# Dilated sliding-window attention and a two-layer MLP: the last four plain output tiles join the groups of seven products, three loads change their queue, and the order is made anew

## The chip, the core and the metric

The kernel runs on one core of a Trainium2 chip. Five engines work side by side and meet at semaphores: TensorE (PE in the profile, its weight loads PEld), VectorE (DVE), ScalarE (ACT), GpSimd (POOL) and SyncE (SP), which here only issues transfers. PE multiplies out of SBUF into eight PSUM banks; DVE and ACT read PSUM, POOL does not. Transfers between HBM and SBUF are carried by 16 DMA engines and are issued by SP or ACT. The metric is the device time of one launch in microseconds.

## The reference

Two stages, with float32 inputs and output. Stage one is attention over 8 batches, 8 heads, 576 tokens and 64 dimensions. Heads 0 to 3 see a window of the last 32 tokens; heads 4 to 7 see every fourth token of the last 128.

```python
scores = scale * q @ k.T                     # per batch and head, 576 x 576
mask_plain = (rel >= 0) & (rel < 32)
mask_dil = (rel >= 0) & (rel < 128) & (rel % 4 == 0)
attn = softmax(where(mask, scores, -1e9)) @ v
```

Stage two takes the 8 x 576 = 4608 tokens with 8 x 64 = 512 features each: `h = x @ w_in` (512 x 2048), `g = max(0.01 h, h)`, `out = g @ w_out` (2048 x 512).

## The kernel before

All operands are cast to fp16 on the chip. The tokens of two batches (1152) are cut into three chunks of 384, so there are 12 chunks, and each chunk has three output tiles of 128 tokens: 36 tiles.

**Attention.** The heads of a batch are handled in pairs, called `vi` 0 to 3; 2 and 3 are the dilated ones and go first (`VISITS`). For batches 0 and 1, q and k are loaded into `stg`, cast into `nat` (L501 on ACT, L502 on DVE or POOL), transposed on PE (L740) and copied into `slots` (L513, L514). v is loaded into `vst` and cast into `slots`. A `unit` (two per pair) multiplies scores (L896, the mask as a bias by L892), takes the exponential on ACT (L904), sums on PE (L921), multiplies with v (L915), takes 1/sum on ACT as a logarithm and an exponential (L940, L942) and normalises on DVE into `xt` (L953). Each unit takes two PSUM banks. The last 64 tokens of a batch go through a buffer `rest` of their own (transposes at L788, `rest_unit`).

**First layer.** `up` (L1054) and `up_pair` (L1088) multiply `w_in` with `xt`, and ACT writes the leaky ReLU into `gt` (L1070). Chunk 0 goes block by block: the products of one head pair can run as soon as that pair's rows of `w_in` and of `xt` are there. Chunk 1 is half batch 0 (first 192 tokens) and half batch 1. The last three chunks (9 to 11) use seven products for eight (`ups7`, L1188).

**Second layer.** It has two forms. `down` makes a plain tile: 16 matmuls of 512 columns (L1268) in four parts, each part waiting only for its four rows of `w_out`; DVE copies the result out (L1276). `group` makes four tiles by Strassen's scheme in Winograd's form: seven products of two halves, each eight matmuls of 256 columns (L1358), with eight sums of activations on DVE (L1344), copies out of PSUM on ACT or DVE (L1387, L1389) and additions on DVE (L1395). It needs four sums of weight blocks (`weight_sums`, L1298), made once when all of `w_out` has been cast; the third overwrites a block of `w_out` in place. The sums of activations use `rest` and `pair1` as buffers; `half_free[0]` makes the first group wait until the transposes of batch 0's and 1's rests have read `rest`:

```python
half_free[0] = raw[0, "rest"][1] + raw[1, "rest"][1]
part_free[0] = part_free[1] = rings["STG"][-1]
```

`PLAIN` says how many tiles are plain before the groups begin: 4, so that there are four plain tiles and eight groups.

**What sets the order.** The kernel first collects all work as tasks with their dependencies and modelled durations (`_Plan`). A forward pass places them on engines and queues by priority; a backward pass from the end gives each its latest start as its new priority; this is repeated `PASSES` times. Then a table `NUDGE` shifts the priorities of single tasks (by task number), and a table `HAND` pins single tasks to an engine. The instructions are written out in the order that results, and each engine runs its own in order. `LATE`, `FAST` and the like are terms of the modelled arrival of transfers; `WHEN` holds first guesses for the times of the batches.

The opening is written out by hand in `FIRST`, a list of steps: `q01` loads q and k of batch 0's head group 1 (heads 4 to 7), `v01` its v, `r0` the rests, `w0` to `w15` the sixteen 512 KB blocks of weights (0 to 7 are `w_in`, 8 to 15 are `w_out`), `c` a mask table. The priority of such a load is the place of its step in the list, shifted by `NUDGE`. Nearly all loads are issued by SP (L486); ACT issues k of `q01` and the identity (`con`). The casts of a weight block go to POOL or DVE, or to ACT as well for the blocks listed in `HELPED`, which is empty. Where PE has nothing to do before its first MLP product, the program fills the planned gap with products of zeros (`warm`, L1472 and L1589).

Of the kernel before, what the change touches and what calls it, by code (L numbers as in the profile page):

```python
# [15 lines left out]
ROOM, LATE, LANDS, SERVE, FSERVE = 256, 1.06, 0.6, 1.1, 1.04  # L16
SOON = 0
FAST = 0.21
WHEN = (3.92, 2.82, 39.64, 80.18, 115.4, 117.81, 161.72, 152.03)
PASSES = 8  # L20
SEVEN = (9, 10, 11)
SECOND = 'st01t'
# [3 lines left out]
HELPED = ()  # L26
TURNS, SCORES, SUMS_, VALUES, UPS, DOWNS = 0, 0, 0, 0, 0, 0
STRETCH = 1.0
FIRST = ('r0 q01 q00 v01 v00 w0 w1 w2 w3 w4 w5 w6 q11 w7 w8 q10 w9 w10 v11 w11 w12 w13 w14 v10 '
         'w15 r1 c')  # L30
NUDGE = {
# [334 lines left out]
def kernel(  # L366
# [14 lines left out]
    B, H, S, D = q.shape  # L381
# [45 lines left out]
    VH = 1152  # L427
# [190 lines left out]
    def load_v(b, g, prio, queue="SP"):  # L618
        base = (b * H + 4 * g) * HS
        vn, v_old = ring("VST", NVS, v_users := [])  # L620
        vs, v_old = vst[vn], v_old + t_blank[vn]
# [26 lines left out]
    w_in_t, w_out_t = {}, {}  # L648
# [1003 lines left out]
```

## Time and profile before

| | us |
|---|---|
| median of 3 runs | 294.82 (294.46 to 295.19) |
| profiled execution, its own time | 296.16 |
| its span | 294.4 |
| PE busy | 284.7 (97%) |
| DVE busy | 225.3 (77%) |
| ACT busy | 218.5 (74%) |
| POOL busy | 124.2 (42%) |

The span runs from the first to the last instruction, so the profiled execution has 1.8 us around it. PE's busy time includes the products of zeros at the start. Rows of a timeline read: start, duration, engine, line of the kernel, operation, what it writes and reads, how many were merged; in brackets the idle time of the engine just before, and what ended it. A row of a stage reads: length, then busy time and count of instructions for each engine, the granted clock of PE as a share, the mean busy share of the 16 DMA engines (a little above 1 when packets overlap), and GB/s.

### The profile page before, as it was taken

How to read it: one execution, taken by the hardware profiler on the slowest of the kernel's cores; microseconds unless marked ns; L12 is line 12 of the kernel's file. 1: busy time of each engine (PE TensorE's matmuls, PEld its weight loads, DVE VectorE, ACT ScalarE, POOL GpSimd, SP SyncE). 2: the span in 40 equal slices, each digit the busy share in tenths (PEclk: the TensorE clock that was granted, in tenths of full speed). 3: DMA queues.
4: the chain of work that ended last, by engine and by line, in shares of the span. 5: the costliest groups of instructions: out<-in, count | busy, mean ns of one | idle time of the engine just before them, and what ended most of it. 6: DMA issues, size and time to landing. Idle time of an engine off the chain costs nothing.

```text
span 294.4 us, 7619 instructions
## 1 busy us (share of the span) xinstructions
PE 284.7 (97%) x2920; PEld 226.3 (77%) x2920; DVE 225.3 (77%) x437; ACT 218.5 (74%) x482; POOL 124.2 (42%) x174
## 2 busy tenths in 40 slices
PE   6879999999999999999999999999999999999995
PEld 2557776686687789677777787887688999999984
DVE  7858397864799879867839879897878889678672
ACT  4967898489859985888978887988767965755521
POOL 4540452656537747874873683653424000000000
PEclk9979999999999999999999999999999999999999
DMA  7999999799788969999798898852001210121133
GB/s 240 275 403 401 394 366 203 156 175 208 128 169 185 170 150 186 199 157 199 198 178 142 195 182 153 197 134 75 31 7 36 75 38 0 38 73 36 38 108 109
DMA packets 156068, 47.15 MB, mean 160 GB/s; under 512 B 136832, under 2 KB 153344, under 8 KB 156032
## 3 DMA queue, kind: packets, MB, share of 16 engines
q1 hardware_dynamic: 155344, 46.04, 64.5%
q10 hardware_dynamic: 688, 0.63, 0.6%
q8 instruction: 23, 0.38, 0.5%
q14 instruction: 13, 0.11, 0.1%
HBM read 37.22 MB, written 9.44 MB: 158 GB/s over the span
## 4 chain that ended last, share of the span: by engine, by line
PE 92%; DMA 3%; DVE 2%; ACT 1%; POOL 0%; issue 0%; ACTq 0%; DVEq 0%; SPq 0%
PE hps L1054 27%; PE fps L1358 23%; PE tp L1358 9%; PE hps L1188 5%; PE fps L1268 4%; PE hps L1088 4%; PE ops L1188 3%; PE ops L915 3%; DMA gt<-in_moe_w_in_dram 2%; PE ops L896 2%; PE ops L921 2%; PE sps L896 2%; PE sps L1188 1%; DMA con<-consts 1%; PE sps L921 1%; PE ops L1358 1%
## 5 line engine op out<-in xcount | busy, mean ns | idle before, releaser
L1054 PE MATMUL hps<-xt,w_in 128*128 128x384 f16 x488 | 94.9, 325 | 2.0 <-POOL w_in L502 2.0
L1358 PEld LDWEIGHTS <-gt 128*128 128x128 f16 x768 | 73.0, 98 | 9.8 <-DVE gt L1344 0.2
L1070 ACT ACTIVATE gt<-hps 128x384 f16<-128x384 f32 x122 | 59.1, 488 | 13.6 <-PE hps L1054 12.7
L1054 PEld LDWEIGHTS <-w_in 128*128 128x128 f16 x512 | 45.0, 98 | 23.3 <-POOL w_in L502 2.1
L502 POOL CAST slots<-vst 128x576 f16<-128x576 f32 x55 | 46.7, 875 | 22.8 <-DMA vst<-in_v_dram 6.8
L502 POOL CAST nat<-stg 128x576 f16<-128x576 f32 (+1 forms) x52 | 36.1, 716 | 47.0 <-DVE gt L1344 18.7
L1358 PE MATMUL fps<-w_out,gt 128*128 128x256 f16 x368 | 46.7, 272 | 0.0
L908 DVE TENSOR_TENSOR ee<-ee,con 128x384 f16<-128x384 f16 (+1 forms) x48 | 20.6, 430 | 15.3 <-ACT ee L904 14.8
L942 ACT ACTIVATE rc<-rc 128x288 f32<-128x288 f32 (+1 forms) x64 | 27.2, 437 | 1.1
L953 DVE TENSOR_TENSOR xt<-ops,rc 128x288 f16<-128x288 f32 (+2 forms) x44 | 19.4, 445 | 10.6 <-ACT rc L942 6.1
L513 ACT COPY slots<-turned 64x512 f16<-64x512 f16 (+1 forms) x30 | 23.9, 800 | 0.8 <-DVE turned L705 0.5
L1211 ACT ACTIVATE gt<-vst 128x384 f16<-128x384 f32 (+1 forms) x24 | 16.0, 684 | 8.0 <-DVE vst L1207 8.0
L896 PEld LDWEIGHTS <-slots 128*128 128x128 f16 x308 | 18.2, 98 | 4.8 <-DVE slots L514 0.5
L514 POOL COPY slots<-turned 64x576 f16<-64x576 f16 (+2 forms) x25 | 16.7, 675 | 12.0 <-ACT slots L513 4.3
L904 ACT ACTIVATE ee<-ops 128x416 f16<-128x416 f32 (+2 forms) x35 | 16.7, 487 | 3.7 <-PE ops L896 3.0
L915 PEld LDWEIGHTS <-slots 128*128 128x128 f16 x308 | 17.4, 98 | 2.4 <-ACT slots L501 0.6
L921 PEld LDWEIGHTS <-con 128*128 128x128 f16 x168 | 14.1, 98 | 6.0 <-issue 1.0
L705 DVE STREAM_TRANSPOSE turned<-nat 128x576 f16<-128x576 f16 x24 | 18.0, 759 | 0.1
L904 ACT ACTIVATE ee<-sps 128x416 f16<-128x416 f32 (+2 forms) x29 | 14.4, 497 | 4.2 <-PE sps L896 3.1
L1387 ACT COPY stg<-fps 128x512 f32<-128x512 f32 (+1 forms) x20 | 10.4, 520 | 9.4 <-PE fps L1358 9.0
L1344 DVE TENSOR_TENSOR gt<-gt 128x1024 f16<-128x1024 f16 x21 | 16.6, 791 | 0.3 <-PE fps L1358 0.2
L1188 PEld LDWEIGHTS <-w_in 128*128 128x128 f16 x192 | 16.2, 98 | 0.2
(157 smaller groups left out, 557.8 us busy)
## 6 DMA issues: line engine op xcount, KB each, us to landing
out_dram<-osb SPq DMA_DIRECT2D x32, 256.0 KB, 2.6
stg<-in_k_dram SPq DMA_DIRECT2D x48, 144.0 KB, 3.5
stg<-in_q_dram SPq DMA_DIRECT2D x48, 144.0 KB, 3.6
vst<-in_v_dram SPq DMA_DIRECT2D x16, 288.0 KB, 4.3
vst<-in_v_dram SPq DMA_DIRECT2D x32, 128.0 KB, 3.2
gt<-in_moe_w_in_dram SPq DMA_DIRECT2D x6, 512.0 KB, 7.4
stg<-in_q_dram SPq DMA_DIRECT2D x3, 512.0 KB, 7.0
stg<-in_k_dram SPq DMA_DIRECT2D x3, 512.0 KB, 9.1
```

What stands on the lines that cost most here:

```text
L502: return ENG[e].tensor_copy(out=dst, in_=src)
L513: return nc.scalar.copy(out=dst, in_=src)
L896: nc.tensor.matmul(p_bank[:, c:c + w], slot(tn, KB + 128 * s, 0, 128, [1, 128]), slot(tn, qx, 0, 128, *qd), start=first or not by_pe, stop ...
L904: lambda e: nc.scalar.activation(out=et[:, 0:n], in_=p_bank[:, 0:n], func=AF.Exp, scale=SCALE), prio)
L908: lambda e: nc.vector.tensor_tensor(out=et[:, 0:n], in0=et[:, 0:n], in1=con[:, table:table + n], op=ALU.mult), prio,
L915: nc.tensor.matmul(at(dst, 0, 128, o, *od), lhs(s), et[:, c:c + w], start=i == 0, stop=i == len(steps) - 1, skip_group_check=True)
L921: nc.tensor.matmul(at(p_bank, 0, 128, o, *od), block_ones, at(et, 0, 128, c, *cd), start=i == 0, stop=i == len(rows) - 1, skip_group_check ...
L942: lambda e: nc.scalar.activation(out=rt, in_=rt, func=AF.Exp, scale=-1.0), prio)
L1054: nc.tensor.matmul(ht[:, 0:n], at(w_in, 0, 128, vi * DFF + j // 2 * 256 + j % 2, [2, 128]), at(xt[m % 2], 0, 128, vi * 1152 + x0 + x, [1, n]),
L1070: lambda e: nc.scalar.activation(out=gt[c % NG][:, j * n_c + x:j * n_c + x + n], in_=ht[:, 0:n], func=AF.Prelu, alpha=0.01),
L1188: nc.tensor.matmul(bk[:, n * i:n * i + n], w(v, 2 * z + i), x(v), start=first and i == 0 and v == 0, stop=i == 1 and v == 1, skip_group_ch ...
L1358: nc.tensor.matmul(bk[:, x:x + HN], tl[:, off + j * step:off + j * step + 128], rhs(j), start=first and x == 0 and j == 0, stop=j == HJ - ...
```

## The change

- `PLAIN` goes from 4 to 0: no plain tile is left, and the 36 tiles are nine groups of four. The first group is made of the four tiles that were plain.
- The first two products of a group wait for the rows of `w_out` that they read (`rows_in`). Before, the weight sums and the plain tiles made sure of that.
- For batch 0, three of the six loads of v of heads 4 to 7 (its second pair of heads, `hh` = 1) are issued by ACT; SP issued them before.
- `HELPED` lists blocks 0, 1 and 2: their casts may run on ACT too.
- `FIRST` starts with `v01`, and loads of batch 1 stand earlier among the weight blocks. `LATE`, `FAST` and `WHEN` have other values, a bank in `SECOND` is another one, and `NUDGE` and `HAND` are new tables, so the order of all the work is new.

```diff
-ROOM, LATE, LANDS, SERVE, FSERVE = 256, 1.06, 0.6, 1.1, 1.04
+ROOM, LATE, LANDS, SERVE, FSERVE = 256, 2.33, 0.6, 1.1, 1.04
-FAST = 0.21
-WHEN = (3.92, 2.82, 39.64, 80.18, 115.4, 117.81, 161.72, 152.03)
+FAST = 0.12
+WHEN = (2.04, 4.98, 44.17, 67.29, 111.43, 110.73, 161.72, 162.22)
-SECOND = 'st01t'
+SECOND = '1t01t'
-HELPED = ()
+HELPED = (0, 1, 2)
-FIRST = ('r0 q01 q00 v01 v00 w0 w1 w2 w3 w4 w5 w6 q11 w7 w8 q10 w9 w10 v11 w11 w12 w13 w14 v10 '
-         'w15 r1 c')
+FIRST = ('v01 r0 q01 q00 v00 w0 w1 w2 w3 w4 w5 q11 w6 w7 q10 w8 v11 w9 w10 w11 v10 w12 w13 w14 '
+         'w15 r1 c')
 NUDGE = {
...
 HAND = {
...
-    def load_v(b, g, prio, queue="SP"):
+    def load_v(b, g, prio):
...
+            queue = "ACT" if b == 0 and hh else "SP"
             c_in = load(queue, every2(vs, hh, VH * hh + 512, [S, 2], [1, D]),
...
-            ab = [load("SP", every2(vs, hh, VH * hh + j * S, [256, 2], [1, 256]),
+            ab = [load(queue, every2(vs, hh, VH * hh + j * S, [256, 2], [1, 256]),
...
-    PLAIN = 4
+    PLAIN = 0
...
-        p1 = product(raw_of(0, 0), w_raw(0, 0), X, True, lambda i: ready(i, 0), 0, 0)
-        p2 = product(raw_of(0, 1), w_raw(1, 0), Y, True, lambda i: ready(i, 1), 1, 0)
+        rows_in = [sum((w_out_t[k * HJ + j] for j in range(HJ)), []) for k in range(2)]
+        p1 = product(raw_of(0, 0), w_raw(0, 0), X, True, lambda i: ready(i, 0) + rows_in[0], 0, 0)
+        p2 = product(raw_of(0, 1), w_raw(1, 0), Y, True, lambda i: ready(i, 1) + rows_in[1], 1, 0)
```

More of the change, by code (lines that the diff above doesn't have):

```diff
@@ L25 @@
 BEHIND = 1.0
-HELPED = ()
+HELPED = (0, 1, 2)
 TURNS, SCORES, SUMS_, VALUES, UPS, DOWNS = 0, 0, 0, 0, 0, 0
 STRETCH = 1.0
-FIRST = ('r0 q01 q00 v01 v00 w0 w1 w2 w3 w4 w5 w6 q11 w7 w8 q10 w9 w10 v11 w11 w12 w13 w14 v10 '
+FIRST = ('v01 r0 q01 q00 v00 w0 w1 w2 w3 w4 w5 q11 w6 w7 q10 w8 v11 w9 w10 w11 v10 w12 w13 w14 '
          'w15 r1 c')
 NUDGE = {
[78 rows of a table removed]
-HAND = {
-    2: "POOL", 3: "POOL", 9: "POOL", 36: "ACT", 37: "DVE", 59: "POOL", 89: "POOL", 91: "POOL", 92:
-    "POOL", 97: "POOL", 111: "POOL", 113: "POOL", 114: "POOL", 139: "DVE", 146: "ACT", 154: "DVE",
-    161: "DVE", 324: "ACT", 331: "DVE", 566: "POOL", 567: "ACT", 573: "DVE", 575: "DVE", 582:
-    "POOL", 727: "ACT", 729: "ACT", 737: "DVE", 892: "DVE", 1001: "POOL", 1004: "POOL", 1059:
-    "POOL", 1149: "ACT", 1167: "POOL", 1314: "DVE", 1322: "DVE", 1352: "DVE", 1588: "ACT", 1598:
-    "DVE", 1623: "POOL", 1629: "POOL", 1633: "ACT", 1728: "DVE", 1740: "DVE"}
[87 rows of a table added]
+HAND = {
+    3: "DVE", 5: "POOL", 8: "DVE", 29: "POOL", 44: "POOL", 46: "POOL", 55: "ACT", 59: "DVE", 61:
+    "DVE", 62: "DVE", 68: "POOL", 70: "DVE", 75: "POOL", 83: "POOL", 91: "POOL", 100: "ACT", 107:
+    "POOL", 111: "POOL", 117: "POOL", 143: "DVE", 144: "DVE", 156: "DVE", 159: "ACT", 161: "ACT",
+    324: "ACT", 330: "DVE", 343: "DVE", 479: "DVE", 517: "DVE", 582: "POOL", 583: "ACT", 591:
+    "POOL", 592: "POOL", 745: "ACT", 750: "POOL", 949: "ACT", 997: "POOL", 1004: "POOL", 1006:
+    "POOL", 1014: "POOL", 1161: "DVE", 1166: "DVE", 1168: "POOL", 1171: "POOL", 1172: "POOL", 1176:
+    "ACT", 1323: "ACT", 1418: "ACT", 1419: "POOL", 1425: "ACT", 1432: "POOL", 1436: "ACT", 1548:
+    "DVE", 1563: "DVE", 1595: "DVE", 1597: "DVE", 1631: "POOL", 1637: "ACT", 1721: "DVE", 1739:
+    "ACT", 1823: "DVE", 1909: "DVE"}
 def _constants():
```

165 rows, old and new, of the table NUDGE are left out of this document.

## The prediction

> **What bounds the kernel now.** I read the page first (sections 1 and 2), then stages, then the chain, then the queues at the start.
>
> ```profile
> span 294.4 us, 7619 instructions
> PE 284.7 (97%) x2920; PEld 226.3 (77%) x2920; DVE 225.3 (77%) x437; ACT 218.5 (74%) x482; POOL 124.2 (42%) x174
> ...
> PEclk9979999999999999999999999999999999999999
> DMA  7999999799788969999798898852001210121133
> ```
>
> TensorE (PE) is busy 97% of the span, the DMA engines are full for the first six slices or so (44 us), and the granted clock dips once, in the third slice. The stages say where PE's time is not work:
>
> ```profile
> core 0: us, PE busy (x) PEld busy (x) DVE busy (x) ACT busy (x) POOL busy (x), PEclk, DMA share, GB/s
> 0.00:12.00 12.00, 8.28 (x60) 4.17 (x61) 9.04 (x17) 6.99 (x15) 5.33 (x13) 1.00 0.89 275
> 12.00:16.00 4.00, 3.66 (x53) 2.56 (x51) 3.89 (x8) 4.00 (x10) 2.77 (x3) 1.00 0.84 245
> 16.00:19.00 3.00, 0.90 (x16) 0.61 (x13) 1.66 (x4) 1.53 (x5) 0.87 (x1) 1.00 1.02 406
> 19.00:22.50 3.50, 3.50 (x28) 2.38 (x27) 1.22 (x3) 2.11 (x6) 1.49 (x2) 0.51 1.02 407
> 22.50:57.50 35.00, 34.69 (x381) 24.81 (x380) 26.50 (x58) 27.48 (x65) 12.73 (x17) 1.00 1.01 310
> 57.50:291.30 233.80, 233.69 (x2401) 191.74 (x2397) 183.03 (x350) 176.04 (x385) 100.98 (x139) 1.00 0.58 124
> ```
>
> From 22.5 us on PE is never without work: 0.31 us idle up to 57.5, 0.11 us after it. What is left to win is multiplications taken out, and the first 22.5 us. A stage in which PE is fed has no slack to give back either: work that arrives late there costs its full length.
>
> **The change part by part.** *1. Four plain tiles become a group.* The chain gives the unit prices, a quarter of a plain tile (four matmuls of 512 columns) and half a product (eight of 256):
>
> ```profile
> 45.26 0.86 PE fps L1268 x4
> ...
> 79.58 0.87 PE fps L1358 x8
> ```
>
> Removed: 4 tiles x 4 quarters x 0.86 = 13.76 us. Added: 7 products x 2 halves x 0.87 = 12.18 us. That is -1.6 us of PE, which counts in full wherever PE is fed. The other eight groups hold the same tiles as before, since the four plain ones were exactly the first four; only their banks alternate the other way round, which I cost at nothing.
>
> *2. The start.* These rows hold it (SPq and ACTq are the engines' DMA issues, the bracket is the idle time before and its releaser):
>
> ```profile
> 1.79 0.49 ACTq L486 DMA_DIRECT2D con<-consts  x1
> 3.88 1.14 ACT L501 CAST nat<-stg 128x512 f16<-128x512 f32 x2 [1.87 <-DMA stg<-in_q_dram]
> 6.87 4.87 SPq L486 DMA_DIRECT2D vst<-in_v_dram  x6
> 11.14 0.62 ACT L501 CAST nat<-stg 128x512 f16<-128x512 f32 x1
> 11.78 2.67 SPq L486 DMA_DIRECT2D gt<-in_moe_w_in_dram  x4
> 11.82 0.40 PE L740 MATMUL tp<-con,nat 128*128 128x128 f16 x4 [0.69 <-ACT nat L501]
> 15.92 0.54 SPq L486 DMA_DIRECT2D stg<-in_k_dram  x1
> 17.84 0.87 POOL L502 CAST w_in<-gt 128x512 f16<-128x512 f32 x1 [2.09 <-DMA gt<-in_moe_w_in_dram]
> 18.77 0.34 PE L1054 MATMUL hps<-xt,w_in 128*128 128x384 f16 x1 [2.01 <-POOL w_in L502]
> ```
>
> PE waits 2.01 us for the first w_in cast. SP issues six v loads in 4.87 us, 0.81 each, ahead of the first weight block at 11.78. Three such loads (batch 0, heads 6 and 7 of v) go to ACT. SP is relieved of 3 x 0.81 = 2.4 us; ACT issues 3 x 0.49 = 1.5 us more. ACT's 1.87 us of waiting ahead of its cast at 3.88 covers that. If the memsets that these loads wait for are late, ACT's cast of q stands behind a blocked issue, and at most the 1.5 us come back as delay.
>
> The weights do not land 2.4 us earlier, because the transfers are the limit: the DMA share is 1.02 once the weights stream, and 0.84 only between 12 and 16 us. Filling that hole is worth 4 x (1.02 - 0.84) / 1.02 = 0.7 us. The new priorities also put block w1 ahead of w0 and one v load of batch 0 behind it: 0.52 MB at 406 GB/s (1.3 us) against 0.29 MB at 275 GB/s (1.1 us), so 0.2 us later. The first half of w0 is cast by ACT (0.62) and no longer by POOL (0.87): 0.25 earlier. Sum: the first matmul with w_in 0.75 us earlier, and PE's gap 1.3 us and no longer 2.0. Bounds: 2.4 earlier (the whole of SP's relief), or none.
>
> Then the clock. From 19 to 22.5 us it was 0.51; 3.5 x 0.49 = 1.7 us are lost. The drop follows the only long gap; the gap of 0.69 before 11.82 was followed by a clock of 1.00. A gap of 1.3 is a little nearer to 0.69 than to 2.01, so I take the drop as gone: -1.7. Bounds: 0 and -1.7. Start together: -2.4, from +1.5 to -4.1.
>
> The Trainium skill, page "TensorE: Matmul & The Clock Gate", section "What's actually happening", has the half rate come after at least one idle window of about 3.4 us; by it neither gap is long enough, the drop has another cause and stays, and the start would be worth 0.7. This trace differs from the page: a gap of 2.01 us went ahead of a half clock.
>
> *3. The cover that goes.* Plain quarters are handed out as w_out arrives, each needing only four of its rows. Where they ran, and the stretch that they filled:
>
> ```profile
> 35.00:57.50 22.50, 11.97 (x48) 4.12 (x48) 1.00 0.98 261
> ...
> 37.36 0.30 PE L892 MATMUL sps<-con 128*128 128x192 f16 x2
> ...
> 38.15 0.61 SPq L486 DMA_DIRECT2D vst<-in_v_dram  x1
> 38.85 2.54 SPq L486 DMA_DIRECT2D xt<-in_moe_w_out_dram  x1
> ...
> 48.78 0.75 DVE L502 CAST w_out<-xt 128x512 f16<-128x512 f32 x2
> 49.45 1.22 DVE L1298 TENSOR_TENSOR wst<-w_out 128x2048 f16<-128x2048 f16 x1
> ...
> 52.73 0.39 PE L788 MATMUL tp<-con,rest 128*128 128x128 f16 x4
> ...
> 57.64 1.48 PE L1088 MATMUL hps<-xt,w_in 128*128 128x192 f16 x16
> ```
>
> The first row counts L1268 alone: 48 of its 64 matmuls, 12 quarters or 10.3 us, lie between 35 and 57.5 us, woven between the units of batch 1's attention (first at 37.36). Only at 57.64 do w_in products with batch 1's tokens begin. Group 0 is less pliant. Its first product needs eight rows of w_out, the second the last eight (cast at 48.78); this is the new dependency `rows_in`. The weight sums start at 49.45, when all of w_out is there. The first sum of activations overwrites the buffer `rest`, which batch 1's last transposes read at 52.73, so product 7 (half of it), 6 and 5 come after that. By 57.5 I expect products 1, 2, 7, 6: 4 x 1.74 = 7.0 us, which leaves 3.3 us uncovered. Bounds: products 1 and 2 alone (6.8 uncovered), all seven (none).
>
> DVE gets eight sums and three additions more and loses four evictions; ACT or DVE gets four evictions:
>
> ```profile
> 49.00:57.50 8.50, 8.19 (x93) 5.17 (x90) 7.93 (x17) 4.70 (x13) 3.49 (x3) 1.00 0.89 164
> ...
> L1344 DVE TENSOR_TENSOR gt<-gt 128x1024 f16<-128x1024 f16 x21 | 16.6, 791 | 0.3 <-PE fps L1358 0.2
> ...
> L1395 DVE TENSOR_TENSOR osb<-tp,stg 128x512 f32<-128x512 f32 x14 | 9.6, 684 | 3.3 <-PE tp L1358 2.1 <-ACT stg L1387 1.1
> ```
>
> That is 8 x 0.79 + 3 x 0.68 - 4 x 0.68 = 5.6 us on DVE and 4 x 0.68 = 2.7 us on either. DVE is busy 7.93 of 8.5 us exactly there, so some of it moves behind 57.5, where PE has w_in products to run instead. I cost it at nothing beyond the 3.3; queued behind it would be batch 1's normalisations, and PE's w_in products wait for those.
>
> *4. Batch 1 earlier.* A load's priority is the place of its step in `FIRST` plus its entry in `NUDGE`; sorted by that, the old numbers give the order that SP's rows show, and the new ones give the order to come. Batch 1's k was issued at 15.92 behind six weight blocks and now stands behind two; its last v (38.15) stood behind fifteen and now stands behind thirteen. Two blocks of 0.52 MB at 406 GB/s are 2.6 us, and the hole filled in step 2 is 0.7: batch 1's tokens are ready 3.3 us earlier. Bounds: 0 (if the units are held by ACT or by banks) and 5.2 (the four blocks that k gains).
>
> *Sum.* Up to batch 1's tokens PE's work is limited by what has arrived: 3.3 uncovered less 3.3 earlier is 0. The 2.4 us won at the start then only lets PE come sooner to the point where it waits, so it is not counted. Left are the -1.6 us of step 1. The tail is the same last group:
>
> ```profile
> 290.37 0.89 PE fps L1358 x8
> ```
>
> The profiled execution took 296.16 us by its own time, 294.4 of it span; the runs without profile have a median of 294.82. I subtract from that: **293.2 us**.
>
> **The rivals.** *A. PE stays fed.* Five or more products fit before batch 1 is ready, or the w_in products kept back from the start fill the hole; the start's 2.4 us count: 294.8 - 1.6 - 2.4 = 290.8. For: over the whole stretch DVE is busy only 26.50 of 35 us. Against: `rest` and the last rows of w_out.
>
> *B. The missing cover makes it slower.* Only products 1 and 2 are ready in the stretch (6.8 uncovered), since DVE's queue, already full there, delays the sums; batch 1 comes 1.3 us earlier: -1.6 + 6.8 - 1.3 = +3.9, 298.7. It decides from the point where uncovered work less batch 1's lead is over 1.6 us. For: 7.93 of 8.5 busy. Against: the start's products can be delayed to fill.
>
> *C. The change does not bring forward what it names.* The transfers are the limit, the loads from ACT queue with SP's, batch 1 gains 1.7 (one block and a bit) for 3.3 uncovered: -1.6 + 1.6 = 0, 294.8. The Trainium skill, "DMA: Bandwidth & Descriptors", section "Issuing engines are not separate DMA queues", says that several issuing engines save only the issue time; the share of 1.02 agrees.
>
> *D. The half clock stays, the rest goes as in A.* 290.8 + 1.7 = 292.5. This is what the page on the clock gate gives; the gap of 2.01 us speaks against its rule, a remaining gap of 1.3 for the outcome.
>
> **How the numbers follow.** Forecast (292.4 to 294): 0.30. A: 0.17. D: 0.13. C: 0.10. B: 0.30. A difference under 0.3% (0.9 us) can't be told from none. Forecast, A and D are faster: 0.60; C is the same: 0.10; B is slower: 0.30. The range begins below A, where more of the start counts (290.0), and ends at 298.0, short of B's full price. The faster cases alone would be 290.0 to 294.0.
>
> **What would show it.** Step 1: sixteen more half products under the group's line, no plain line, PE's busy time after 60 us at its old rate. Step 2: the first w_in matmul at about 18.0, no slice with a clock under 0.9. Step 3: idle time of PE between 42 and 57 us, ended by DVE or ACT; none would be A, over 4 us B. Step 4: the first w_in products with batch 1's tokens at about 54. It is wrong if the start stalls elsewhere (ACT's q cast late behind its own issues), if a gap in the middle brings the clock down a second time, or if the new order breaks the feeding after 60 us, where 0.11 us of idleness leaves nothing to improve.

## The result, and the profile after

| | before | after |
|---|---|---|
| median of the runs side by side (7 each) | 295.19 us (294.46 to 296.40) | 297.79 us (296.20 to 298.26) |
| profiled execution, its own time | 296.16 | 297.79 |
| its span | 294.4 | 296.0 |

The ratio is 1.0079 (95% interval 1.0053 to 1.0105): the changed kernel is 0.8% slower. A later comparison on another chip (run e5 below) gave 1.0093 (1.0056 to 1.0131). I had forecast 293.2 us, faster. To read the spans: most executions of the kernel before (51 of the 73 whose clock is on record) have a mean clock of 0.998 or more and spans around 293, ten of eleven of the changed kernel are under 0.995; but each of the two profiled executions holds one stretch at half clock (before from 19.0 to 22.5 us, after from 15.3 to 18.8), so these two compare like with like.

The page of the changed kernel, sections 1, 2 and 4:

```profile
span 296.0 us, 7729 instructions
PE 284.0 (96%) x2961; PEld 231.9 (78%) x2961; DVE 219.1 (74%) x435; ACT 219.0 (74%) x491; POOL 129.2 (44%) x178
...
PEclk9979999999999999999999999999999999999999
...
PE 83%; DVE 5%; DMA 4%; ACT 4%; issue 1%; SPq 1%; POOL 0%
```

PE's busy time is 0.7 us less than before (284.7), and the span is 1.6 us more. The busy time includes the zero products at the start, but these take about the same in both (3.54 us before, 3.60 after). In the chain that ended last, other engines and the queues hold 17%. The stages say where PE waits; the same windows of the changed kernel, cut as in the prediction:

```profile
0.00:12.00 12.00, 7.64 (x49) 4.26 (x49) 7.83 (x16) 5.53 (x10) 5.44 (x14) 1.00 0.79 233
12.00:16.00 4.00, 1.73 (x25) 1.41 (x24) 1.88 (x5) 2.02 (x6) 1.62 (x2) 0.92 0.96 269
16.00:19.00 3.00, 2.79 (x24) 1.96 (x23) 2.44 (x5) 2.58 (x6) 2.62 (x4) 0.54 0.93 265
19.00:22.50 3.50, 3.06 (x39) 2.14 (x36) 1.79 (x5) 3.37 (x8) 2.17 (x4) 1.00 1.02 368
22.50:57.50 35.00, 33.80 (x435) 28.25 (x432) 25.86 (x54) 31.24 (x80) 13.90 (x19) 1.00 0.99 318
57.50:293.00 235.50, 235.00 (x2404) 193.82 (x2402) 178.90 (x354) 174.25 (x384) 103.49 (x139) 1.00 0.60 127
```

Up to 22.5 us PE is idle for 7.28 us (before: 6.16), between 22.5 and 57.5 for 1.20 (before: 0.31), after that for 0.50 (before: 0.11). That is 1.1, 0.9 and 0.4 us more; with 0.7 us less of busy time, and 0.1 us less behind PE's last product, it makes up the 1.6 us of the span. Finer windows, for the kernel before first and the changed kernel second:

```profile
25.00:45.00 20.00, 20.00 (x204) 15.06 (x201) 14.42 (x33) 17.27 (x39) 7.77 (x12) 1.00 1.07 380
45.00:57.50 12.50, 12.19 (x133) 7.68 (x131) 10.25 (x23) 8.14 (x20) 4.96 (x6) 1.00 0.91 178
57.50:70.00 12.50, 12.50 (x145) 9.99 (x142) 6.04 (x13) 10.78 (x23) 7.84 (x12) 1.00 0.96 182
```

```profile
25.00:45.00 20.00, 19.52 (x218) 15.00 (x216) 13.57 (x32) 18.69 (x46) 9.04 (x12) 1.00 1.05 371
45.00:57.50 12.50, 11.85 (x166) 11.12 (x164) 10.68 (x19) 10.15 (x29) 4.44 (x6) 1.00 0.90 218
57.50:70.00 12.50, 12.05 (x119) 9.51 (x118) 11.03 (x18) 7.28 (x15) 8.60 (x10) 1.00 0.85 161
```

PE's idle time from 25 to 70 us is 0.31 us before and 1.58 us after. DVE is the engine that changed most: from 57.5 to 70 us its busy time went from 6.04 to 11.03 us. The start, from the timeline of the changed kernel (issues of ACT and SP, and PE):

```profile
4.17 2.00 ACTq L498 DMA_DIRECT2D vst<-in_v_dram  x3
```

```profile
5.65 0.55 SPq L498 DMA_DIRECT2D gt<-in_moe_w_in_dram  x1
...
9.31 4.97 SPq L498 DMA_DIRECT2D vst<-in_v_dram  x2
14.33 0.60 SPq L498 DMA_DIRECT2D gt<-in_moe_w_in_dram  x1
```

```profile
15.48 0.61 PE L753 MATMUL fps<-con,nat 128*128 128x128 f16 x4 [1.93 <-DVE nat L514]
...
20.17 0.34 PE L1067 MATMUL hps<-xt,w_in 128*128 128x384 f16 x1
```

The three loads went to ACT as meant, but SP gained nothing: w0 goes out at 14.33 us (before, the first weight block, w0, went out at 11.78), and the first product with w_in starts at 20.17 (18.77 before).

### The profile page after: what moved, and what is told of

It reads as the page before. It is cut to its first block, busy times and chain, and to the rows that moved or that the text cites. A ratio compares the mean times of both kernels' runs of the same rounds, so it can differ in the third digit from the quotient of the medians.

```text
span 296.0 us, 7729 instructions
## 1 busy us (share of the span) xinstructions
PE 284.0 (96%) x2961; PEld 231.9 (78%) x2961; DVE 219.1 (74%) x435; ACT 219.0 (74%) x491; POOL 129.2 (44%) x178
## 4 chain that ended last, share of the span: by engine, by line
PE 83%; DVE 5%; DMA 4%; ACT 4%; issue 1%; SPq 1%; POOL 0%
PE hps L1067 26%; PE fps L1371 24%; PE tp L1371 9%; PE hps L1201 5%; PE ops L1201 3%; DMA stg<-in_q_dram 3%; PE ops L928 2%; PE ops L909 2%; DMA stg<-in_k_dram 2%; PE ops L934 2%; PE sps L909 1%; PE sps L1201 1%; ACT slots L525 1%; PE sps L934 1%; PE ops L1371 1%; DVE gt L1357 1%
## 5 line engine op out<-in xcount | busy, mean ns | idle before, releaser
L1371 PEld LDWEIGHTS <-gt 128*128 128x128 f16 x864 | 81.7, 98 | 11.1 <-issue 0.3
L1083 ACT ACTIVATE gt<-hps 128x384 f16<-128x384 f32 x122 | 58.3, 489 | 15.3 <-PE hps L1067 14.3
L1067 PEld LDWEIGHTS <-w_in 128*128 128x128 f16 x512 | 45.8, 98 | 24.0 <-issue 1.5
L514 POOL CAST slots<-vst 128x576 f16<-128x576 f32 x59 | 52.0, 909 | 20.3 <-DVE ee L942 3.9
L1371 PE MATMUL fps<-w_out,gt 128*128 128x256 f16 x416 | 53.5, 272 | 0.0
L955 ACT ACTIVATE rc<-rc 128x288 f32<-128x288 f32 (+1 forms) x64 | 26.3, 435 | 0.6
L1400 ACT COPY stg<-fps 128x512 f32<-128x512 f32 (+1 forms) x25 | 13.5, 542 | 14.2 <-PE fps L1371 12.6
L526 POOL COPY slots<-turned 64x576 f16<-64x576 f16 (+2 forms) x25 | 15.7, 631 | 10.5 <-DVE turned L718 4.5
L1371 PE MATMUL fps<-wst,gt 128*128 128x256 f16 x144 | 18.3, 272 | 0.0
L1357 DVE TENSOR_TENSOR gt<-gt 128x1024 f16<-128x1024 f16 x24 | 17.5, 737 | 0.1
L1371 PE MATMUL tp<-w_out,gt 128*128 128x256 f16 x136 | 17.5, 272 | 0.1
```

The lines of the kernel that those rows point to most:

```text
L514: return ENG[e].tensor_copy(out=dst, in_=src)
L955: lambda e: nc.scalar.activation(out=rt, in_=rt, func=AF.Exp, scale=-1.0), prio)
L1067: nc.tensor.matmul(ht[:, 0:n], at(w_in, 0, 128, vi * DFF + j // 2 * 256 + j % 2, [2, 128]), at(xt[m % 2], 0, 128, vi * 1152 + x0 + x, [1, n]),
L1083: lambda e: nc.scalar.activation(out=gt[c % NG][:, j * n_c + x:j * n_c + x + n], in_=ht[:, 0:n], func=AF.Prelu, alpha=0.01),
L1357: lambda e: ENG[e].tensor_tensor(out=dst, in0=a, in1=b, op=op),
L1371: nc.tensor.matmul(bk[:, x:x + HN], tl[:, off + j * step:off + j * step + 128], rhs(j), start=first and x == 0 and j == 0, stop=j == HJ - ...
```

## The experiments

Kernels sent together are compared with runs of the kernel before on the same chip. In e2, e3, e4, e7 and e11 the order of every engine's queue was written out, and the few tasks that changed were fitted in where there was room; the code shown is then the part that matters, and "..." stands for what is left out. A row of waits reads: who waited for whom, us in total, times, longest us.

**e1: the queue alone.**

```diff
-        eng = ENG[queue]
+        eng = ENG["SP" if -1500 < prio < -1498 else queue]
```

> The changed kernel with its order kept, but the three loads of v that went to ACT are issued by SP again, in the same places. If the order of the transfers is what counts (my theory), this stays within 0.3% of the changed kernel (about 297.5 us by its median) and the first matmul with w_in stays at 20 us. If the queue is what cost (ACT's issues take places among the transfers in flight that SP's weights then wait for), block w1 goes out at about 3.2 us and not at 5.65, and 1 us or more comes back.

Measured: 296.31 us (296.21 to 297.09), ratio 1.0056 (1.0039 to 1.0072). Putting the loads back on SP doesn't bring the kernel to the level of before. Against the 1.0079 of the changed kernel the intervals overlap, so this run alone doesn't show that the queue costs anything; the comparison on one chip is e5 and e6.

**e2: the plain tiles back, in the changed kernel's order.** The plain quarters take the places of group 0's products, and the third weight sum stands behind them.

```diff
...
-    PLAIN = 0
+    PLAIN = 4
...
```

> The changed kernel with every engine's order kept, but the first four tiles plain again: sixteen plain quarters stand where the fourteen half products stood (up to 72 us), the third weight sum behind them. If group 0's stiffness makes PE wait, the waits between 45 and 70 us (together about 2 us in the changed kernel) go, and the time is that of the changed kernel or up to 0.5 us less in spite of 1.6 us more of columns. If the order of the loads makes PE wait, the waits at 33 to 40 us stay at about 1.4 us, and the time is about 1.5 us above the changed kernel.

Measured: 300.09 us (299.20 to 301.22), ratio 1.0171 (1.0136 to 1.0206). Its windows:

```profile
25.00:45.00 20.00, 19.51 (x211) 14.40 (x209) 13.25 (x30) 18.83 (x45) 9.02 (x12) 1.00 1.01 349
45.00:57.50 12.50, 12.50 (x154) 9.92 (x153) 8.42 (x14) 9.04 (x26) 4.78 (x6) 1.00 1.03 247
57.50:70.00 12.50, 12.50 (x102) 7.63 (x99) 5.25 (x11) 7.72 (x16) 6.05 (x9) 1.00 0.81 171
```

From 45 to 70 us PE no longer waits at all: the waits there belong to group 0. DVE's load falls with them (8.42 and 5.25 us). The time is nevertheless longer. Behind 70 us two waits of 0.8 and 0.6 us appear, both ended by DVE, which now has the late third sum and the last plain tile's copy to do beside batch 2's work; that this is the whole reason is not shown. So e2 settles the place of the cause and not its price.

**e3: group 0 in the order of before.**

```diff
...
-    PLAIN = 4
+    PLAIN = 0
...
```

> The kernel before with every engine's order kept, but group 0 for the plain tiles: its products go where their inputs are there and PE's next task is later. If the missing cover is what costs, PE waits for 4 to 7 us between 38 and 58 us where the kernel before waits for 0.5, and the time is 298 us or more. If the cover is not needed and only the loads' order was bad, PE waits for less than 1.5 us there and the time is at or under that of the kernel before.

Measured: 306.41 us (305.40 to 307.59), ratio 1.0384 (1.0345 to 1.0423). The middle window and the waits of PE from 22.5 to 72 us:

```profile
45.00:57.50 12.50, 7.52 (x86) 5.97 (x86) 10.43 (x20) 6.38 (x16) 5.67 (x7) 0.86 0.92 182
```

```profile
PE ops L1411 <- DVE xt L1374: 3.6, 1, 3.6
PE ops L1313 <- DVE xt L1374: 1.9, 2, 1.5
PE ops L1313 <- DVE slots L935: 1.4, 1, 1.4
```

Without the plain quarters PE has 5.0 us of nothing in those 12.5 us. In this order the cover was worth more than the 3.3 us that I gave it; the order of the change avoids most of that. The whole 11.5 us are not the hole's price: the granted clock is 0.86 in this window and 0.86 again from 57.5 to 70 us, which is 2 x 12.5 x 0.14 = 3.5 us at half clock (an estimate from these two rows), and all four executions have a mean clock of 0.989. A hole in the middle with half clock around it is what the prediction named as a sign of being wrong; in the changed kernel it did not come.

**e4: batch 1's early loads undone.** Three loads of q and k of batch 1 go behind the last w_in block, so that w_in comes first as it did before; the rest of batch 0's and 1's work is fitted in around them. In the kernel's table of starts the three (72, 73, 85) now stand behind the last block of w_in to go out (66):

```python
66: (18.52, "SP"), ... 72: (18.64, "SP"), 73: (18.62, "SP"), ... 85: (18.63, "SP")
```

> The changed kernel with the loads of batch 1's q and k behind the last four blocks of w_in, and the work up to the first group placed anew by the same priorities. If late w_in blocks make the waits at 33 to 36 us (0.8 us), those go; batch 1 is then later by three blocks (4 us), and I expect its units to make PE wait about as long or longer between 43 and 52 us: 297 to 300 us. If the waits at 33 to 36 us have another cause they stay.

Measured: 301.81 us (301.05 to 302.37), ratio 1.0225 (1.0195 to 1.0256). From 45 to 57.5 us PE is busy for 11.07 us (11.85 in the changed kernel). This speaks for batch 1's early arrival: without plain quarters, later tokens mean a longer hole. But batch 1's first w_in products start only 1.2 us later (53.84 against 52.66), and part of the price may come from the work fitted in anew and from the clock (a mean of 0.988 or 0.989 in three of the four executions), so it is no clean number.

**e5 and e6: the changed kernel, and with v back on SP, on one chip.** The edit of e6 is that of e1.

> The changed kernel beside the next three, on one chip. All theories: 297.8 us within 0.5, ratio to the kernel before 1.006 to 1.011. It gives the price against which the next run is read.

> The changed kernel with the three loads of v back on SP, as before, beside the changed kernel itself. Theory (loads of SP and ACT share eight places, each waiting for the load eight places earlier, so that loads issued by ACT keep w1 and w0 back): 1.2 to 1.8 us faster than the changed kernel, first product with w_in near 18.0 against 20.2. Rival (the later start of the w_in products is made up for by the waits of 33 to 70 us, so the queue costs nothing): within 0.5 us of the changed kernel.

Measured: 298.19 us (297.82 to 298.93), ratio 1.0093, and 296.77 us (295.60 to 298.33), ratio 1.0043 (1.0012 to 1.0074): moving the queue costs 1.4 us. Part of that may be the half clock, which came with it: the mean clock was under 0.995 in all four executions of e5 and in one of ten of e6. Against this, the profiled execution of e5 has two such stretches (0.987) and a span of 296.0, the same as the changed kernel's first with one (0.993). The share stays open. SP's rows and the first w_in product of e6:

```profile
3.16 0.63 SPq L498 DMA_DIRECT2D gt<-in_moe_w_in_dram  x1
...
9.47 2.31 SPq L498 DMA_DIRECT2D vst<-in_v_dram  x2
11.83 0.60 SPq L498 DMA_DIRECT2D gt<-in_moe_w_in_dram  x1
```

```profile
17.63 0.34 PE L1067 MATMUL hps<-xt,w_in 128*128 128x384 f16 x1
```

With three loads more on SP its first weight block goes out 2.5 us earlier (3.16 against 5.65), w0 2.5 us earlier, and the first product starts at 17.63 and not at 20.17. The longest of SP's waits in the changed kernel up to 60 us, 2.5 us, is this one, for a load of q:

```profile
SPq L498 <- DMA stg<-in_q_dram: 3.2, 2, 2.5
```

The reason is in the waits of the compiled program. In it, loads of SP and ACT take eight completion counters (DMAHW0 to DMAHW7) in turn, and a load whose counter was used before waits until the load that used it has landed. From the changed kernel's queues:

```
SP
4 L498 DMA gt_89<-in_moe_w_in_dram 128x1x1024 [waits DMAHW1_49]
5 L498 DMA vst_73<-in_v_dram 64x2x64 [waits DMAHW3_49,DVE_49]
6 L498 DMA vst_73<-in_v_dram 64x2x256 [waits DMAHW4_49]
ACT
6 L498 DMA vst_73<-in_v_dram 64x2x256 [waits DVE_49]
7 L498 DMA vst_73<-in_v_dram 64x2x256
8 L498 DMA vst_73<-in_v_dram 64x2x64 [waits DMAHW2_49]
```

Two of ACT's three loads stand ahead of w1 (SP's row 4) in the turn and take the last free counter and the first one again. So w1 gets the second one and has to wait for a load of q. With v on SP w1 gets the last free counter.

**e7: the queue alone, in the kernel before.**

```diff
...
+            queue = "ACT" if b == 0 and hh else "SP"; ...
...
```

> The kernel before, every engine's order kept, with the three loads of v (batch 0, heads 6 and 7) issued by ACT behind its second cast: the queue's part of the change alone. Theory (shared places): the first product with w_in no earlier than 18.8 us, the time 0 to 2 us longer. Rival, step 2 of the prediction (SP relieved of 2.4 us): w0 issued at 9.4 and not at 11.8, first product with w_in at 18.0 or before, the time 0.7 to 2.4 us shorter.

Measured: 295.95 us (294.97 to 296.96), ratio 1.0009 (0.9987 to 1.0030): no difference. Three of its rows, SP's first weight blocks, the first w_in product, and the window behind them:

```profile
11.31 4.01 SPq L904 DMA_DIRECT2D gt<-in_moe_w_in_dram  x4
```

```profile
18.30 0.33 PE L1472 MATMUL hps<-xt,w_in 128*128 128x384 f16 x1
```

```profile
25.00:45.00 20.00, 18.71 (x185) 14.06 (x184) 12.75 (x29) 16.33 (x37) 7.16 (x11) 1.00 1.07 383
```

Three loads less in SP's queue bring w0 forward by 0.5 us (11.31 against 11.78), not by 2.4. And the small lead, with no half clock in it, turns into 1.29 us of idle time between 25 and 45 us, where the kernel before has none: the lead at the start is lost again by 45 us.

**e8: DVE's sums made thin.** Six subtractions of group 0 and, by a like edit, the third weight sum work on a quarter of their columns, in the same order. The kernel leaves out the rest of these sums, so its output is another one.

```diff
...
-                    lambda e: ENG[e].tensor_tensor(out=dst, in0=a, in1=b, op=op),
+                    lambda e, m=HJ // 4 if op == ALU.subtract and len(seen) == 1 else HJ: ENG[e].tensor_tensor(
+                        out=dst[:, :m], in0=a[:, :m], in1=b[:, :m], op=op),
...
```

> The changed kernel with the six in-place subtractions of activations of group 0 and the third weight sum done on a quarter of their columns (so the output is another one); the order is the same. DVE has 4 to 4.5 us less to do between 50 and 63 us. Theory (DVE, full there with the sums that group 0 brings, delays batch 1's normalisations and group 0's own products): the idle time of PE between 50 and 70 us falls from 1.6 to under 0.6 us, the time by 0.8 to 1.5 us. Rival (PE lacks work there whatever DVE does: products 7, 6, 5 come behind the transposes that read rest, and ACT's chain sets batch 1): idle time over 1.2 us, the time within 0.4 us.

Measured: 296.38 us (295.64 to 297.43), ratio 1.0031 (1.0007 to 1.0056), which is 1.8 us faster than the changed kernel on the same chip. From 57.5 to 70 us:

```profile
57.50:70.00 12.50, 12.50 (x132) 10.53 (x130) 7.91 (x16) 8.13 (x17) 6.47 (x10) 1.00 0.86 164
```

PE's idle time of 0.45 us there is gone once DVE's busy time falls from 11.03 to 7.91. The rival, that PE lacks work there whatever DVE does, falls for this order.

**e9: DVE relieved without leaving anything out.** v is on SP. One copy out of PSUM (task 479) and four casts of batch 2's q and k (539 to 542) go to ACT; POOL made those casts beside DVE's sums. The fourth weight sum (463) stands behind batch 1's last normalisations (411, 412), one w_out cast (125) behind a normalisation (390).

```diff
...
+    moved = {479: ('ACT', 51.9), 539: ('ACT', 55.1), 541: ('ACT', 55.75), 540: ('ACT', 58.3), 542: ('ACT', 58.9),
+             411: ('DVE', 56.6), 412: ('DVE', 56.61), 480: ('DVE', 56.9), 463: ('DVE', 58.47),
+             390: ('DVE', 44.95), 125: ('DVE', 45.26)}
...
```

> The changed kernel with the three v loads back on SP, and DVE relieved by other means, the output unchanged: one copy out of PSUM of group 0 and four casts of batch 2's q and k (which POOL did beside DVE's sums) go to ACT, the fourth weight sum stands behind batch 1's last normalisations, one w_out cast behind a normalisation. Theory (DVE's queue between 46 and 63 us is what PE waits for): the waits of 0.3, 0.6 and about 0.35 us at 47, 55.5 and 61 us go; 0.8 to 1.3 us faster than with v on SP alone: 295.5 to 296.0, ratio to the kernel before 1.000 to 1.003. Rival (ACT's chain is the limit there, and casts on ACT stand ahead of its leaky ReLU copies): no gain, 296.6 or more.

Measured: 294.80 us (294.18 to 296.50), ratio 0.9984 (0.9950 to 1.0017). That is better than expected, 1.7 us less than e6 by the ratios (1.0043 less 0.9984, of 295; the two ran on different chips, and their intervals overlap by a little), and level with the kernel before. Its windows:

```profile
25.00:45.00 20.00, 19.67 (x224) 15.81 (x222) 12.57 (x30) 19.14 (x46) 8.44 (x12) 1.00 1.00 356
45.00:57.50 12.50, 12.14 (x167) 11.17 (x165) 11.03 (x19) 9.96 (x28) 2.17 (x4) 1.00 0.90 180
57.50:70.00 12.50, 12.50 (x120) 9.87 (x118) 8.45 (x16) 11.04 (x23) 6.86 (x11) 1.00 0.89 174
```

ACT takes on work (7.28 us from 57.5 to 70 in the changed kernel, 11.04 here) and has room for it. DVE's own instructions also get shorter. The third and fourth weight sums and batch 1's last normalisations in the changed kernel, and then the third sum and the normalisations in e9:

```profile
56.05 1.68 DVE L1311 TENSOR_TENSOR w_out<-w_out 128x2048 f16<-128x2048 f16 x1
...
61.00 1.68 DVE L1311 TENSOR_TENSOR t<-w_out,wst 128x2048 f16<-128x2048 f16 x1
62.60 0.56 DVE L1042 TENSOR_TENSOR xt<-ops,rc 128x128 f16<-128x128 f32 x2
```

```profile
52.65 1.21 DVE L1311 TENSOR_TENSOR w_out<-w_out 128x2048 f16<-128x2048 f16 x1
...
57.24 0.57 DVE L1042 TENSOR_TENSOR xt<-ops,rc 128x128 f16<-128x128 f32 x2 [0.97 <-PE ops L1013]
```

The third sum takes 1.68 us while POOL casts beside it (two casts from 55.91 to 58.26) and 1.21 us when POOL is idle; the normalisations come 5.4 us earlier and now wait for PE, not behind DVE's sums. About 2 us of that lead come with v on SP, since in e6 they stand at 60.94. But it is not always DVE that gets longer. In the kernel before, two such sums ran beside POOL's casts:

```profile
54.01 4.83 POOL L502 CAST nat<-stg 128x576 f16<-128x576 f32 x4 [6.30 <-DMA stg<-in_k_dram]
```

```profile
54.70 1.21 DVE L1298 TENSOR_TENSOR wst<-w_out,wst 128x2048 f16<-128x2048 f16 x1
...
56.50 1.21 DVE L1298 TENSOR_TENSOR t<-w_out,wst 128x2048 f16<-128x2048 f16 x1
```

There the sums kept 1.21 us, and POOL's casts took 1.21 each (4.83 / 4), where such a cast has a mean of 0.72 over that kernel. The Trainium skill, page "Advanced Engine Details and Errata", section "Mode Summary", says that VectorE's second SBUF port is shared with GPSIMD, so that GPSIMD instructions and VectorE's two-port instructions block each other. The rows agree in that one of the two gets longer; the mode of these sums is in no row, and what decides which of the two is held up is not shown.

**e10: v on SP and thin sums together.** The edits of e6 and e8.

> The changed kernel with the three v loads back on SP and, as in the thin sums, six in-place subtractions of group 0 and the third weight sum on a quarter of their columns (the output is another one). Theory (two separate causes, the queue 1.4 to 1.6 us and DVE's sums 1.4 to 1.8 us): they add, 295.0 within 0.4, ratio to the kernel before about 0.999. Rival (each only moves the same wait): no better than either alone, 296.3 or more.

Measured: 295.84 us (294.38 to 297.22), ratio 1.0017 (0.9987 to 1.0047): by the median lower than either alone (1.0043 and 1.0031), and less gain than their sum would give. All three intervals overlap, so neither is shown, and whether the two causes overlap stays open.

**e11: thin sums in e3.**

> The kernel before, its order kept, group 0 in place of the four plain tiles where it fits, with the same thin sums (the output is another one): against 306.4 with full sums. Theory (DVE's queue delays batch 1's normalisations): 3 to 5 us faster, 301.5 to 303.5, the wait of 3.6 us on a normalisation under 1.5. Rival, step 3 of the prediction (PE lacks cover whatever DVE does): within 1.5 us of 306.4, the same waits with other releasers.

Measured: 305.20 us (two executions, 304.32 and 306.07), ratio 1.0309 (1.0200 to 1.0417), against 306.41 and 1.0384 in e3. The longest wait of PE from 40 to 72 us:

```profile
PE ops L1411 <- DVE xt L1374: 2.9, 1, 2.9
```

Here the rival holds: with DVE relieved most of the hole stays (2.9 us of 3.6). So in the order of before PE lacks cover, and in the order of the change DVE's queue is what is late (e8). A normalisation as the releaser doesn't by itself say that DVE is the cause.

**e12: two moves more on e9.** Two activation sums stand behind the last w_out casts and behind batch 1's normalisations, one cast of `nat` goes to POOL.

```diff
...
+             466: ('DVE', 47.21), 468: ('DVE', 48.515), 86: ('POOL', 31.1)
```

> The relieved kernel (v on SP, POOL's and DVE's work partly on ACT) with two more moves: the two activation sums ahead of product 2 stand behind the last w_out casts and behind batch 1's normalisations, and one cast of batch 1's nat goes from DVE to POOL. Theory (the waits left are DVE's, 0.3 us at 48 us and up to 0.3 us at 32 us): 0.3 to 0.6 us faster than the relieved kernel, 294.2 to 294.5, ratio to the kernel before 0.996 to 0.999. Rival (PE stands there for work that has not arrived, and the wait comes back later): 294.6 to 295.2, ratio 0.998 to 1.001.

Measured: 295.04 us (294.18 to 296.01), ratio 0.9982 (0.9955 to 1.0009): nothing beyond e9, as the rival had it. No version of these beats the kernel before by a measurable amount.

## Why the prediction was wrong, step by step

I forecast 1.6 us less, and the kernel takes 2.6 us more by the medians, 1.6 by the two profiled executions. Two terms that the prediction's sum had at nothing are the ones that failed: the start (step 2), where the move of the loads costs 1.4 us, and DVE's queue behind group 0's sums (in step 3), which is worth 1.7 to 1.8 us. The saving of step 1 did not show in full either.

**Step 1, the multiplications (-1.6 us).** The unit prices hold in the chain: the last half product has 0.89 us in the changed kernel, as it had before:

```profile
292.08 0.89 PE ops L1371 x8
```

By busy time the saving is about half. The second layer's own lines take 16.08 us (plain tiles) and 110.91 (groups) before and 126.15 after, 0.84 less, and PE as a whole has 0.7 less. A row's busy time includes the overlap with the row ahead, so this is no clean price either, and no run isolates the term. In e9, where the two costs below are relieved, the ratio is 0.9984, which is 0.5 us and not 1.6. e9 has 0.69 us of idle time from 25 to 70 us where the kernel before has 0.31; the rest of the difference stays open. The "sixteen more half products" of the last part of the prediction is a slip: seven products of two halves are fourteen, and the trace has fourteen more (1008 matmuls under the group's line, 896 before).

**Step 2, the start (-2.4 us, not counted in the sum). This step failed, also in its sign.** I took SP's relief as 3 x 0.81 us and bounded the first w_in product by the transfers: 18.0 us forecast, 20.17 measured. What I didn't see is that in the compiled program a load can wait for the landing of an earlier load, of either queue. In the changed kernel the loads on ACT push w1 from 3.16 to 5.65 and w0 from 11.83 to 14.33 (e6 and after). Price to the end: 1.4 us (e5 and e6), with an open share of the half clock in it. My upper bound (+1.5, the cast of q standing behind ACT's issues) had about the size, but from another mechanism, so that is luck. That a lead at the start isn't worth counting was right for the 0.5 us of e7, which are lost again by 45 us. A delay was not absorbed the same way in the changed kernel; why not is not isolated.

The clock argument failed too. I let the half clock hang on the length of the gap before it, and expected no slice under 0.9; there is one, at 0.7, behind a gap of 1.93 us at another place. A long gap is not needed for it. In the windows from 12 to 16 us of e6 and of e9, which open alike and in which PE has no gap over 1 us ahead of it from 6 us on, one has it and the other doesn't:

```profile
12.00:16.00 4.00, 3.11 (x40) 2.16 (x39) 3.56 (x8) 4.00 (x12) 1.81 (x3) 1.00 1.11 335
```

```profile
12.00:16.00 4.00, 3.82 (x37) 2.96 (x38) 3.35 (x8) 4.00 (x12) 2.17 (x4) 0.61 1.12 351
```

Nor does the gap's length settle how often it comes: ten of eleven executions of the changed kernel have a mean clock under 0.995 (a gap of 1.93 us in its opening), 22 of 73 of the kernel before (2.01), and two of the nineteen of e1 and e6 (0.59, as far as e6's trace shows). So the order of the opening bears on it, but by what is open. The -1.7 of the profile was hardly the change's to win: the three runs whose median I subtracted from are 1.0 to 1.7 us shorter than the profiled execution, as executions without the stretch are (their clock is not on record).

**Step 3, the cover (3.3 us uncovered, DVE at nothing). The lower bound of the products came, and the nothing was wrong.** By 57.5 us only products 1 and 2 have run, not 1, 2, 7 and 6:

```profile
44.23 1.04 PE L1371 MATMUL fps<-w_out,gt 128*128 128x256 f16 x8
...
45.28 1.04 PE L1371 MATMUL fps<-w_out,gt 128*128 128x256 f16 x8
...
50.69 1.91 PE L1371 MATMUL fps<-w_out,gt 128*128 128x256 f16 x16
...
57.78 1.91 PE L1371 MATMUL tp<-w_out,gt 128*128 128x256 f16 x16
```

That is my lower bound, 6.8 us uncovered. DVE, "busy 7.93 of 8.5 us exactly there", does the sums from 49 to 63 us without a break, several of them slower beside POOL's casts (from 56 us on), and batch 1's last normalisations come at 62.60 behind them. I had named that queue and priced it at nothing; e8 puts it at 1.8 us, e6 and e9 at 1.7. Idle time from 42 to 57 us was to show the step right or wrong; 0.45 of the 1.10 us that PE is idle from 45 to 70 us came behind 57.5, where I had stopped looking.

**Step 4, batch 1 earlier (3.3 us).** The outcome came, and more of it, just under the bound of 5.2:

```profile
52.66 2.26 PE L1101 MATMUL hps<-xt,w_in 128*128 128x192 f16 x24
```

Forecast was about 54, and 57.64 was before: 5.0 us earlier. The mechanism that I gave for it is not what the loads show. Batch 1's k was issued at 15.74 us (15.92 before); its other early loads of q and k went out 1.9 to 4.1 us sooner, but its last v at 38.00 and not at 38.15, though it stood behind twelve weight blocks (I had counted thirteen) and not fifteen. So the load that comes last explains 0.15 of the 5.0 us. The earlier k and q give a part: e4, which issues the first k 3.7 us later, has the products 1.2 us later. By 57.5 us PE also has 6.8 us less of second-layer work to do between batch 1's units, which can bring them forward; no run separates the two. The loads that stand ahead keep the last w_in blocks back: 0.3 us of PE's 0.48 us of idle time from 25 to 45 us ends with a cast of w_in by DVE.

**The sum.** The prediction's terms give -1.6 (step 1) + 1.4 (queue) + 6.8 - 5.0 (cover less lead) = +1.6, and the spans of the two profiled executions differ by +1.6. That agreement is no proof and in part luck: two terms are my own bounds and not measurements, step 1 shows about half its size by busy time, and the 6.8 and the 5.0 may be partly the same work, counted once as a loss and once as a lead. What the profiles show without them is the idle time: +1.1 us before 22.5, +0.9 up to 57.5, +0.4 after. Of the rivals, B is the nearest: it had the mechanism ("DVE's queue, already full there, delays the sums") and 298.7 us; I gave it the same chance as the forecast. Its time is partly luck too, since it had batch 1 earlier by 1.3 us and not 5.0, and no cost of the queue. That cost stands nearest to C ("the loads from ACT queue with SP's"), which had no delay from it.

## What to carry to other kernels

Work that fills a hole is worth its flexibility as well as its length: sixteen quarters that need four rows each could run in any gap, seven products that need sums from a full engine could not. Before moving a load to another queue, look at what the load waits for besides its queue: if the program gives the queues common completion counters, as here, the other queue's loads still stand in line. And when an engine is busy 93% of the time exactly where the new work lands, price its queue; the remedy that kept the output was to move its neighbours' work (ACT had room) and to put what can wait behind what is waited for.

## What the runs showed of the hardware

- In these compiled programs, loads issued by SP and by ACT wait in one rotation of eight counters: moving three from SP to ACT made SP's first weight block leave 2.5 us later (5.65 against 3.16 us).
- An issue can hold SP for long: two v loads in a row took 4.97 us in the changed kernel and 2.31 us in e6, against 0.60 for a weight block. The second of them also waits for a counter in the compiled program, so what the issue itself takes of that is not shown.
- A DVE subtraction of 128 x 2048 values takes 1.21 us alone, and 1.68 us beside POOL's casts in the changed kernel; in the kernel before it kept 1.21 us beside them, and POOL's casts took 1.21 us each and not 0.72.
- The half clock comes in stretches of about 3.4 us (an estimate from e9's clock, 0.61 over 4 us and 0.95 over the next 3), at different places in executions of like instructions, and without a gap of PE over 1 us ahead of it (e9). Two executions of the same kernel, the changed one, have one stretch and two (mean clock 0.993 and 0.987) and the same span, 296.0.
